# A segment loop with streamed weights: four stream buffers and 13 slices in place of five and 14, and the output columns split 256 + 384

## The chip, the cores and the metric

The kernel runs on one core of one Trainium2 chip. The metric is the device time of one execution in microseconds. TensorE (PE) multiplies and writes to PSUM, VectorE (DVE) and ScalarE (ACT) copy and compute, GpSimd (POOL) does a little, and SyncE (SP) and ScalarE issue the DMA transfers, which run on 16 DMA engines.

## The reference

`x` has 2048 rows of 640. Part A cuts it into 64 segments of 32 rows and carries 8 rows of memory from one segment to the next, so the segments form a chain:

```python
for s in range(n_seg):
    h = jnp.concatenate([mem, xs], axis=1)        # 8 + 32 rows
    q, k, v = h @ Wq, h @ Wk, h @ Wv              # each 640 -> 32 heads x 192
    p = softmax(where(mask, q k^T * scale, -1e9)) # 40 x 40 per head
    o = (p v) @ Wo                                # 6144 -> 640
    mem = o[:, :M, :]                             # the next segment's memory
    outs.append(o[:, M:, :])
```

Part B is a local attention with window 8 and dilation 2 over all 2048 rows. The result is `g * a + (1 - g) * b` with a gate `g` for each row.

## The kernel before, in words

Three stages run one after the other. `part_b` computes part B and stores it to DRAM. `prepass` projects those rows of each segment that do not depend on the chain. `part_a` is the loop over 64 segments that this text is about; `part_z` at the end finishes some output rows of all segments.

The four weight matrices do not fit into on-chip memory. Most of them is resident. What is not is cut into slices of 128 x 1536 bf16 (384 KB), listed in `STREAM` (L15). A slice of a projection is named by matrix, column unit and row chunk: `("q", 1, 1)` is unit 1 (512 columns of each quarter) of row chunk 1 of `Wq`. The five row chunks are the five blocks of 128 of the 640 inputs. A slice `("oa", i)` or `("ob", i)` is a piece of `Wo`: `oa` is the part that makes the first output columns, `ob` the rest. In every segment all 14 slices are read again from a copy in DRAM (`wscr`). `get_unit` (L565) takes one of `WBUFS` buffers of the pool `wst` and issues the transfer on SyncE's queue (L569); the transfer waits until TensorE has done its last matmul on the slice that was in that buffer.

Within a segment the order of TensorE, ScalarE and VectorE is written out by hand. `project` (L768) adds up one unit over row chunks: for each chunk four matmuls of 512 columns that run side by side, one for each quarter of the columns. `m_qk(i, chunks)` does this for the units of q (even i) and k (odd i), `c_qk(i)` copies the sum out of PSUM on ScalarE, `t_qk` transposes it, `s_a` and `s_b` make scores, `m_v` and `c_v` do the units of v, and `pv_half(h)` multiplies by the values for one half of the heads. `o_group(part, i2)` (L927) does four matmuls side by side against `Wo`; twelve groups make one part.

At the end of a segment ScalarE copies the finished output to `whi` (L1032 for the first part, L1040 for the second), and `sel` (L948) picks the 8 memory rows out of it with one small matmul for each of the row chunks that the part covers (L953). VectorE copies them to `hT` for the next segment (L956). The first part covers three row chunks and the second two, so the next segment starts its first units with chunks 0, 1 and 2, before the second `sel` has been done. `tail` (L1045) starts the matmuls of `ps_a` for the 24 or so remaining rows; the start of `ps_a` is a handy mark of a segment. Between the halves ScalarE also issues the store of `oz_dram` (L1025), and after L1032 the load for the next segment (`load_z`, L753).

The large sums of a segment take turns in two PSUM banks: the pool `psm` has two buffers under one tag (L748), and an allocation takes the one used before the last.

Of the kernel before, what the change touches and what calls it, by code (L numbers as in the profile page):

```python
# [11 lines left out]
F32 = mybir.dt.float32  # L12
I32 = mybir.dt.int32

STREAM = (("k", 0, 2), ("q", 1, 1), ("k", 1, 2), ("q", 2, 1), ("q", 2, 4), ("k", 2, 4), ("v", 0, 0), ("v", 1, 0), ("v", 1, 3),  # L15
          ("v", 2, 2), ("oa", 0), ("ob", 0), ("oa", 5), ("ob", 7))
N_EARLY = 22
N_COPY = 4
N_MID = 4
N_V = 8  # L20
N_LAST = 4
ZVB = 4
WBUFS = 5

_DEV = {"mode": "full"}

# [3 lines left out]
class _K:  # L30
# [466 lines left out]
    def weights_setup(self):  # L497
        nc, tc, KC = self.nc, self.tc, self.KC
        rest = []
        for m in "qkv":  # L500
            ks = sorted(range(KC), key=lambda kc: (len(self.units(m, 0, kc)) < 3, kc)) if m == "k" else range(KC)
            rest += [(m, J, kc) for kc in ks for J in range(4)]
        rest += [k for k in [("oa", i) for i in range(12)] + [("ob", i) for i in range(8)] if k not in STREAM]
        n = (0, N_EARLY, -N_MID - N_V - N_LAST, -N_V - N_LAST, -N_LAST, None)
        self.early, *self.late = [rest[n[x]:n[x + 1]] for x in range(5)]
        self.W = {m: W.rearrange("(c p) f -> p c f", p=128) for m, W in zip("qkv", (self.Wq, self.Wk, self.Wv))}
        self.wres = self.ctx.enter_context(tc.tile_pool(name="wres", bufs=1))
        self.res_tiles = {}
        self.ahead = {}
        self.after = mybir.DependencyInfo(mybir.DependencyClass.Sync, mybir.DependencyReason.DATA)  # L510
        self.wstream = self.ctx.enter_context(tc.tile_pool(name="wstream", bufs=WBUFS))
        self.wscr = dict(zip(STREAM, self.dram.tile([len(STREAM), 128, 1536], BF, name="wscr")))

    def tile_of(self, pool, k):
        n = 1536 if k[0] in ("oa", "ob") else 512 * len(self.units(*k))
        t = pool.tile([128, n], BF, name="w_" + "_".join(map(str, k)))
        self.res_tiles[k] = t if n < 1536 or k[0] in ("q", "k", "v") else t[:].rearrange(
            "p (c f) -> p c f", c=4 if k[0] == "oa" else 6)
        return t

    def load_res(self, k, t):
# [10 lines left out]

    def wo_slice(self, k, dst):

        n, f0, f1 = (4, 0, 384) if k[0] == "oa" else (6, 384, 640)
        src = self.Wo.rearrange("(c p) f -> p c f", p=128)[:, :, f0:f1]
        return dst.rearrange("p (c f) -> p c f", c=n), src[:, n * k[1]:n * k[1] + n]

    def wo_place(self, part, c):

        n = 4 if part == "oa" else 6
        return c // n, c % n

    def res(self, m, J, kc, c0, n):
# [175 lines left out]
    def part_a(self):  # L720
        nc, tc, KC, S = self.nc, self.tc, self.KC, self.S
        nseg = S // self.seg
        scale_a = float(self.Dh) ** (-0.5)
        ctx = ExitStack()
        with ctx:
# [19 lines left out]
            oTxs = [v.rearrange("p (c q) -> p c q", q=32) for v in V]  # L745
            a4 = ZB[:, 1536:1696]

            psm = ctx.enter_context(tc.tile_pool(name="psm", bufs=2, space=bass.MemoryType.PSUM, reuse_waits="tile"))  # L748
            psx = ctx.enter_context(tc.tile_pool(name="psx", bufs=2, space=bass.MemoryType.PSUM, reuse_waits="tile"))
            psS = ctx.enter_context(tc.tile_pool(name="psS", bufs=2, space=bass.MemoryType.PSUM, reuse_waits="tile"))  # L750

# [13 lines left out]
            for s in range(nseg):  # L765
                pqs, sts, pTs, pSs = {}, {}, {}, {}

                def project(ps, m, u, kcs):  # L768
                    for kc in kcs:
                        st = self.get_unit((m, u, kc)) if (m, u, kc) in STREAM else None  # L770
                        for j in range(4):
                            rhs = self.res(m, j, kc, 512 * u, 512) if st is None or j == 3 else st[:, 512 * j:512 * j + 512]
                            nc.tensor.matmul(ps[32 * j:32 * j + 32, :], lhsT=hT[:, kc, :], rhs=rhs, start=(kc == 0),  # L773
                                             stop=(kc == KC - 1), tile_position=(0, 32 * j), skip_group_check=True)

                def m_qk(i, kcs):
                    if i not in pqs:
                        pqs[i] = psS.tile([128, 2, 512], F32, tag="S", name="ps_qk")[:, 0, :] if i == 1 else \
                            psm.tile([128, 512], F32, tag="m", name="ps_qk")
                    project(pqs[i], ("q", "k")[i % 2], i // 2, kcs)  # L780

                def c_qk(i):
# [92 lines left out]

                def m_v(u, kcs=range(KC)):
                    if u not in pvs:
                        pvs[u] = psm.tile([128, 512], F32, tag="m", name="ps_v")
                    project(pvs[u], "v", u, kcs)

                def c_v(u):
# [43 lines left out]
                pso = {}  # L925

                def o_group(part, i2):  # L927
                    n = 384 if part == "oa" else 256
                    if i2 == 0:
                        pso[part] = psm.tile([128, 512], F32, tag="m", name="ps_wo")  # L930
                    for jj in range(4):
                        c = order[4 * i2 + jj]
                        J, g, t = c // 12, c // 3 % 4, c % 3
                        i, x = self.wo_place(part, c)
                        if (part, i) not in osl:
                            if s + 1 == nseg and sum(k[0] in ("oa", "ob") for k in STREAM) > WBUFS and i2 == 0 and part == "oa":
                                w = self.res_tiles[self.oz_free.pop()]
                                nc.sync.dma_start(w[:], self.wscr[part, i])
                            else:
                                w = self.get_unit((part, i))  # L940
                            osl[part, i] = w[:].rearrange("p (c f) -> p c f", c=4 if part == "oa" else 6)
                        nc.tensor.matmul(pso[part][32 * jj:32 * jj + 32, 0:n],  # L942
                                         lhsT=oTxs[2 * (g // 2) + J // 2][:, 6 * (J % 2) + 3 * (g % 2) + t, :],
                                         rhs=osl[part, i][:, x, :],
                                         start=(i2 == 0), stop=(i2 == 11),
                                         tile_position=(0, 32 * jj), skip_group_check=True)

                def sel(part, hT_next, pm):  # L948

                    m0, m1 = (0, 3) if part == "oa" else (3, KC)  # L950
                    p = 0 if part == "oa" else 1
                    for m in range(m0, m1):
                        nc.tensor.matmul(pm[:, p, 8 * (m - m0):8 * (m - m0) + 8], lhsT=whi[:, m * 128:(m + 1) * 128],  # L953
                                         rhs=self.sel_m[:], start=(m == m0), stop=(m == m1 - 1),
                                         skip_group_check=True)
                    nc.vector.tensor_copy(hT_next[:, m0:m1, 0:8], pm[:, p, 0:8 * (m1 - m0)].rearrange(  # L956
                        "p (m i) -> p m i", i=8))

                m_qk(0, (0, 1, 2))
                m_qk(1, (0, 1))  # L960
                if sel_b is not None:
                    sel_b()
                m_qk(1, (2,))
                if tail is not None:
                    tail()
                m_qk(0, (3, 4)); c_qk(0)
                m_qk(1, (3, 4)); c_qk(1)
                if store is not None:
                    store()
                m_qk(2, range(KC)); c_qk(2)  # L970
                m_qk(3, range(KC)); c_qk(3)
                m_qk(4, (0, 1))
                for i in range(4):
# [44 lines left out]
                c_z(0, pos, (1, 3), "aa")  # L1018
                c_z(0, pos, (0, 2), "dd")
                for i2 in range(6):  # L1020
                    o_group("oa", i2)
                pos = pv_half(1)
                c_x(1, pos, range(4), "adda")
                c_z(1, pos, range(4), "adad")
                nc.scalar.dma_start(self.oz_dram[s], zst)  # L1025
                if s + 1 == nseg:
                    self.sort_oz(0)
                for i2 in range(5):
                    o_group("ob", i2)
                for i2 in range(6, 12):  # L1030
                    o_group("oa", i2)
                nc.scalar.copy(whi[:, 0:384], pso["oa"][:, 0:384])  # L1032
# [56 lines left out]
    def part_z(self, psm, wo, tail):  # L1089
# [6 lines left out]
        for n in range(4):  # L1096
            b4 = self.res_tiles[free.pop(0)][:, 0:640]
            rows = lambda ap: ap.rearrange("(n s t) f -> n s t f", n=4, t=32)[n, :, 24:32, :]
            nc.scalar.dma_start(b4, rows(self.bsc_dram))
            for part, f0, nf in (("oa", 0, 384), ("ob", 384, 256)):  # L1100
                ps = psm.tile([128, 512], F32, tag="m", name="ps_z")
# [73 lines left out]
```

## Time and profile before

| What | Value |
|---|---|
| median of 3 runs | 1704.7 us (1703.22 to 1705.23) |
| the profiled execution | 1702.23 us, span 1700.5 us |
| TensorE busy | 1600.5 us, 94% of the span |
| granted TensorE clock, mean | 0.983 |
| read from HBM, written | 432.76 MB, 47.23 MB |
| transfers `wst<-wscr` | 896 of 384 KB, on SyncE's queue |
| the segment loop | from about 358 us to about 1640 us of the span |

The page gives busy times of the engines over the whole span and over 40 slices of it. Of the loop, 1282 us for 64 segments, a segment takes about 20 us. The chain of waits follows the work that ended last back to the start; a row with DMA in it is time between a transfer's issue and its landing. Idle time of an engine is listed with what ended it.

### The profile page before, as it was taken

What the parts mean: (1) busy time and instruction counts of PE and PEld (TensorE: products, weight loads), DVE (VectorE), ACT (ScalarE), POOL (GpSimd) and SP (SyncE); (2) the same over time, 40 slices, a digit from 0 to 9 for tenths busy, and PEclk for the clock granted to TensorE, in tenths of its full rate; (3) what the DMA queues carried; (4) which work ended last, traced back from release to release, by engine and by line L of the source; (5) the groups of instructions that cost most, each with busy time, mean ns of one, the idle gap of its engine ahead of it and who ended that gap; (6) DMA issues with size and microseconds to landing.
All of it is one profiled execution on the core that took longest, in us unless ns stands there. A gap on an engine that the chain in (4) does not pass through costs nothing.

```text
span 1700.5 us, 75713 instructions
## 1 busy us (share of the span) xinstructions
PE 1600.5 (94%) x33209; PEld 887.1 (52%) x33209; DVE 700.9 (41%) x2223; ACT 804.5 (47%) x2082; POOL 59.8 (4%) x124
## 2 busy tenths in 40 slices
PE   7887999989999999999999999999999999999989
PEld 4544544445555555555555555555555555555559
DVE  3665333234434444443344434434444434444430
ACT  3877422234444444444445444445454444454450
POOL 2030000000000000000000000000000000000000
PEclk9999899999999999999999999999999999999999
DMA  7798798889989999998999989999999999999981
GB/s 202 186 209 216 227 312 232 257 245 305 305 301 311 305 303 313 300 313 288 300 314 313 308 288 309 318 299 320 304 321 306 306 300 304 307 309 309 306 274 31
DMA packets 307608, 479.44 MB, mean 282 GB/s; under 512 B 100556, under 2 KB 186444, under 8 KB 307276
## 3 DMA queue, kind: packets, MB, share of 16 engines
q1 hardware_dynamic: 208144, 418.12, 75.8%
q10 hardware_dynamic: 99132, 56.46, 11.8%
q8 instruction: 260, 4.26, 1.0%
q14 instruction: 72, 0.59, 0.1%
HBM read 432.76 MB, written 47.23 MB: 282 GB/s over the span
## 4 chain that ended last, share of the span: by engine, by line
PE 85%; DMA 6%; ACT 3%; issue 3%; DVE 1%; SPq 1%; ACTq 0%; DVEq 0%
PE ps_qk L773 25%; PE ps_v L773 13%; PE ps_wo L942 13%; PE ps_pre L622 6%; PE ps_qkT L794 5%; PE ps_S L827 5%; PE ps_oT L899 3%; PE ps_z L1106 3%; PE ps_pre L652 3%; DMA wst<-wscr 2%; PE ps_S L859 2%; PE ps_bqk L236 2%; ACT ZB L1032 2%; DMA bqkT<-bqk_dram 1%; PE ps_mem L953 1%
## 5 line engine op out<-in xcount | busy, mean ns | idle before, releaser
L773 PEld LDWEIGHTS <-hT 128*32 128x32 bf16 x11520 | 277.2, 97 | 287.0 <-issue 18.6
L786 ACT CAST TZ<-ps_qk 128x512 bf16<-128x512 f32 x384 | 218.7, 587 | 315.3 <-PE ps_qk L773 315.3
L773 PE MATMUL ps_qk<-w_q,hT 128*32 128x512 bf16 x3264 | 267.9, 383 | 1.8 <-issue 1.6
L773 PE MATMUL ps_qk<-w_k,hT 128*32 128x512 bf16 x3264 | 266.0, 380 | 2.4 <-issue 2.0
L773 PE MATMUL ps_v<-w_v,hT 128*32 128x512 bf16 x3072 | 245.5, 384 | 0.0
L805 DVE COPY ZB<-ps_qkT 128x512 bf16<-128x512 bf16 (+1 forms) x256 | 91.0, 356 | 349.4 <-PE ps_qkT L794 253.7
L942 PEld LDWEIGHTS <-TZ 128*32 128x32 bf16 x6144 | 146.0, 96 | 110.4 <-ACT TZ L913 39.9
L883 DVE CAST TZ<-ps_v 128x512 bf16<-128x512 f32 (+1 forms) x256 | 136.9, 556 | 45.5 <-PE ps_v L773 45.5
L942 PE MATMUL ps_wo<-w_oa,TZ 128*32 128x384 bf16 x2560 | 147.4, 330 | 7.3 <-issue 6.8
L773 PE MATMUL ps_qk<-wst,hT 128*32 128x512 bf16 x1152 | 149.0, 381 | 0.8 <-DMA wst<-wscr 0.8
L913 ACT CAST TZ<-ps_oT 128x192 bf16<-128x192 f32 x256 | 75.9, 322 | 129.7 <-PE ps_oT L904 83.8
L942 PE MATMUL ps_wo<-w_ob,TZ 128*32 128x256 bf16 x2304 | 108.2, 275 | 14.0 <-issue 13.9
L956 DVE CAST hT<-ps_mem 128x24 bf16<-128x24 f32 x126 | 22.5, 179 | 227.6 <-PE ps_mem L953 227.6
L913 DVE CAST TZ<-ps_oT 128x192 bf16<-128x192 f32 x256 | 85.8, 355 | 57.7 <-PE ps_oT L904 55.8
L773 PE MATMUL ps_v<-wst,hT 128*32 128x512 bf16 x768 | 100.7, 387 | 9.0 <-DMA wst<-wscr 8.9
L794 PE MATMUL ps_qkT<-ident,TZ 128*128 128x128 bf16 x1536 | 107.3, 219 | 0.0
L794 PEld LDWEIGHTS <-TZ 128*128 128x128 bf16 x1536 | 88.6, 98 | 26.9 <-issue 26.9
L942 PE MATMUL ps_wo<-wst,TZ 128*32 128x256 bf16 (+1 forms) x1280 | 96.9, 302 | 4.8 <-issue 4.4
L845 ACT ACTIVATE TZ<-ps_S 32x224 bf16<-32x224 f32 x256 | 89.3, 349 | 13.0 <-PE ps_S L836 10.7
L845 ACT ACTIVATE ZB<-ps_S 32x224 bf16<-32x224 f32 x256 | 89.2, 348 | 13.0 <-PE ps_S L836 9.3
L754 POOL COPY TZ<-ZB 128x384 bf16<-128x384 bf16 x64 | 32.5, 507 | 1467.4 <-DMA ZB<-zpk_dram 565.1
L827 PE MATMUL ps_S<-ZB,TZ 64*128 64x160 bf16 (+1 forms) x704 | 78.1, 234 | 0.0
(135 smaller groups left out, 2037.6 us busy)
## 6 DMA issues: line engine op xcount, KB each, us to landing
wst<-wscr SPq DMA_DIRECT2D x896, 384.0 KB
zpk_dram<-ZS ACTq DMA_DIRECT2D x4, 3072.0 KB
ZB<-zpk_dram ACTq DMA_DIRECT2D x64, 192.0 KB
zpk_dram<-ZV ACTq DMA_DIRECT2D x32, 192.0 KB
TZ<-zpk_dram ACTq DMA_DIRECT2D x64, 96.0 KB
oz_dram<-TZ ACTq DMA_DIRECT2D x64, 96.0 KB
w_q<-in_A_Wq_dram SPq DMA_DIRECT2D x14, 384.0 KB
w_k<-in_A_Wk_dram SPq DMA_DIRECT2D x14, 384.0 KB
```

Of the source, the lines that this page charges most:

```text
L622: nc.tensor.matmul(ps[:], lhsT=weights(j, kc, 6 * Rp + 3 * r + t), rhs=zTi[:, kc, :], start=(kc == 0), stop=(kc == KC - 1))
L652: mm = nc.tensor.matmul(pss[g][:], lhsT=zTi[:, kc, 128 * st:128 * st + 128], rhs=weights(kc, g), start=(kc == 0), stop=(kc == KC - 1))
L773: nc.tensor.matmul(ps[32 * j:32 * j + 32, :], lhsT=hT[:, kc, :], rhs=rhs, start=(kc == 0), stop=(kc == KC - 1), tile_position=(0, 32 * j), ...
L786: nc.scalar.copy(sts[i], pqs[i][:])
L794: nc.tensor.transpose(pT[:, 128 * t:128 * t + 128], st[:, 128 * t:128 * t + 128], self.ident[:])
L805: nc.vector.tensor_copy(QTf[:, run[2]:run[2] + 4, run[3]:run[3] + n, :].rearrange("p b x i -> p x b i"), src.rearrange("p (x b i) -> p x b ...
L827: nc.tensor.matmul(grid(h, par)[:, :, 0:80].rearrange("p j (b r i) -> p j b r i", r=2, i=8)[:, :, :, r, :], lhsT=KTs[3 * R + t][k0:k1, :], ...
L845: nc.scalar.activation(E[ps], pSs[h][ps, :, 112 * j:112 * j + 112], ACT.Exp, scale=scale_a)
L883: nc.vector.tensor_copy(VU[u][:, f0:f1], pvs[u][:, f0:f1])
L899: nc.tensor.matmul(out[:, r, t, :], lhsT=Vt[6 * h + 3 * r + f0 // 128][ks, f0 % 128:f0 % 128 + f1 - f0], rhs=E[ks, par, 0:80].rearrange("p ...
L913: cp(oTxs[2 * h + j // 2][:, 6 * (j % 2):6 * (j % 2) + 6, :], pos[j][:, 0:240].rearrange("p (c q) -> p c q", q=40)[:, :, 8:40])
L942: nc.tensor.matmul(pso[part][32 * jj:32 * jj + 32, 0:n], lhsT=oTxs[2 * (g // 2) + J // 2][:, 6 * (J % 2) + 3 * (g % 2) + t, :], rhs=osl[pa ...
```

## The change

`WBUFS` goes from 5 to 4, and `STREAM` from 14 slices to 13, other ones, in the order in which a segment uses them. The output columns are split 256 + 384 (`oa` has two row chunks, `ob` three) where it was 384 + 256, so a slice of `oa` holds six blocks of `Wo` and one of `ob` four. In a segment the first six groups of `ob` now come before the second `pv_half`, then all twelve of `oa`, the copy of 256 columns, four groups of `ob`, the first `sel`, the last two groups of `ob`, and the copy of 384 columns.

Since the first `sel` gives only chunks 0 and 1, the next segment starts three units with these (q 0, k 0, and chunk 0 of q 1) before the second `sel`, where it started two units with chunks 0, 1, 2 and 0, 1. A unit may thus take its chunks in parts between other units; `done` counts them. The two PSUM banks get a tag each, `m` and `n`, and `bank` names which one a sum takes.

```diff
-STREAM = (("k", 0, 2), ("q", 1, 1), ("k", 1, 2), ("q", 2, 1), ("q", 2, 4), ("k", 2, 4), ("v", 0, 0), ("v", 1, 0), ("v", 1, 3),
-          ("v", 2, 2), ("oa", 0), ("ob", 0), ("oa", 5), ("ob", 7))
+STREAM = (("q", 1, 1), ("q", 1, 2), ("k", 1, 3), ("q", 2, 2), ("k", 2, 2), ("v", 0, 0), ("v", 1, 0), ("v", 1, 2), ("v", 2, 1),
+          ("ob", 0), ("oa", 0), ("oa", 5), ("ob", 8))
...
-WBUFS = 5
+WBUFS = 4
...
-        n, f0, f1 = (4, 0, 384) if k[0] == "oa" else (6, 384, 640)
+        n, f0, f1 = (6, 0, 256) if k[0] == "oa" else (4, 256, 640)
...
-            psm = ctx.enter_context(tc.tile_pool(name="psm", bufs=2, space=bass.MemoryType.PSUM, reuse_waits="tile"))
+            psm = ctx.enter_context(tc.tile_pool(name="psm", bufs=1, space=bass.MemoryType.PSUM, reuse_waits="tile"))
...
+                def bank(n, name):
+                    return psm.tile([128, 512], F32, tag="mn"[(s + n) % 2], name=name)
+
+                done = {}
+
                 def project(ps, m, u, kcs):
                     for kc in kcs:
+                        n = done[m, u] = done.get((m, u), 0) + 1
...
-                            nc.tensor.matmul(ps[32 * j:32 * j + 32, :], lhsT=hT[:, kc, :], rhs=rhs, start=(kc == 0),
-                                             stop=(kc == KC - 1), tile_position=(0, 32 * j), skip_group_check=True)
+                            nc.tensor.matmul(ps[32 * j:32 * j + 32, :], lhsT=hT[:, kc, :], rhs=rhs, start=(n == 1),
+                                             stop=(n == KC), tile_position=(0, 32 * j), skip_group_check=True)
...
-                            psm.tile([128, 512], F32, tag="m", name="ps_qk")
+                            bank(i == 2 or i == 4, "ps_qk")
...
-                        pvs[u] = psm.tile([128, 512], F32, tag="m", name="ps_v")
+                        pvs[u] = bank(u != 1, "ps_v")
...
-                        pso[part] = psm.tile([128, 512], F32, tag="m", name="ps_wo")
+                        pso[part] = bank(part == "oa", "ps_wo")
...
-                    m0, m1 = (0, 3) if part == "oa" else (3, KC)
+                    m0, m1 = (0, 2) if part == "oa" else (2, KC)
...
-                m_qk(0, (0, 1, 2))
+                m_qk(0, (0, 1))
                 m_qk(1, (0, 1))
+                m_qk(2, (0,))
                 if sel_b is not None:
                     sel_b()
-                m_qk(1, (2,))
+                m_qk(2, (1,))
                 if tail is not None:
                     tail()
-                m_qk(0, (3, 4)); c_qk(0)
-                m_qk(1, (3, 4)); c_qk(1)
+                m_qk(0, (2, 3, 4)); c_qk(0)
+                m_qk(1, (2, 3, 4)); c_qk(1)
...
-                m_qk(2, range(KC)); c_qk(2)
+                m_qk(2, (2, 3, 4)); c_qk(2)
...
                 for i2 in range(6):
-                    o_group("oa", i2)
+                    o_group("ob", i2)
                 pos = pv_half(1)
...
-                for i2 in range(5):
-                    o_group("ob", i2)
-                for i2 in range(6, 12):
+                for i2 in range(12):
                     o_group("oa", i2)
-                nc.scalar.copy(whi[:, 0:384], pso["oa"][:, 0:384])
+                nc.scalar.copy(whi[:, 0:256], pso["oa"][:, 0:256])
...
-                for i2 in range(5, 12):
+                for i2 in range(6, 12):
                     o_group("ob", i2)
-                    if i2 == 8 and s + 1 < nseg:
+                    if i2 == 9 and s + 1 < nseg:
                         sel("oa", hT_next, pm)
-                nc.scalar.copy(whi[:, 384:640], pso["ob"][:, 0:256])
+                nc.scalar.copy(whi[:, 256:640], pso["ob"][:, 0:384])
```

In `part_z` the two parts are 256 and 384 columns wide, in this order, in the banks `n` and `m`. The resident weights change in size to match: of the early loads some hold one unit more or fewer.

More of the change, by code (lines that the diff above doesn't have):

```diff
@@ L502, in weights_setup @@
             rest += [(m, J, kc) for kc in ks for J in range(4)]
-        rest += [k for k in [("oa", i) for i in range(12)] + [("ob", i) for i in range(8)] if k not in STREAM]
+        rest += [k for k in [("oa", i) for i in range(8)] + [("ob", i) for i in range(12)] if k not in STREAM]
         n = (0, N_EARLY, -N_MID - N_V - N_LAST, -N_V - N_LAST, -N_LAST, None)
@@ L517, in tile_of @@
         self.res_tiles[k] = t if n < 1536 or k[0] in ("q", "k", "v") else t[:].rearrange(
-            "p (c f) -> p c f", c=4 if k[0] == "oa" else 6)
+            "p (c f) -> p c f", c=6 if k[0] == "oa" else 4)
         return t
@@ L539, in wo_place @@
     def wo_place(self, part, c):
-        n = 4 if part == "oa" else 6
+        n = 6 if part == "oa" else 4
         return c // n, c % n
@@ L927, in o_group @@
                 def o_group(part, i2):
-                    n = 384 if part == "oa" else 256
+                    n = 256 if part == "oa" else 384
                     if i2 == 0:
-                        pso[part] = psm.tile([128, 512], F32, tag="m", name="ps_wo")
+                        pso[part] = bank(part == "oa", "ps_wo")
                     for jj in range(4):
@@ L940, in o_group @@
                                 w = self.get_unit((part, i))
-                            osl[part, i] = w[:].rearrange("p (c f) -> p c f", c=4 if part == "oa" else 6)
+                            osl[part, i] = w[:].rearrange("p (c f) -> p c f", c=6 if part == "oa" else 4)
                         nc.tensor.matmul(pso[part][32 * jj:32 * jj + 32, 0:n],
@@ L1099, in part_z @@
             nc.scalar.dma_start(b4, rows(self.bsc_dram))
-            for part, f0, nf in (("oa", 0, 384), ("ob", 384, 256)):
-                ps = psm.tile([128, 512], F32, tag="m", name="ps_z")
+            for part, f0, nf in (("oa", 0, 256), ("ob", 256, 384)):
+                ps = psm.tile([128, 512], F32, tag="m" if f0 else "n", name="ps_z")
                 for c in range(48):
```

## The prediction

> **What bounds the kernel now.** I read the page first (busy shares, the slices, the chain's shares), then the stretches of the loop, then the chain and the timelines of one segment, and last who waits on the DMA queue.
>
> ```profile
> PE 1600.5 (94%) x33209; PEld 887.1 (52%) x33209; DVE 700.9 (41%) x2223; ACT 804.5 (47%) x2082; POOL 59.8 (4%) x124
> PE   7887999989999999999999999999999999999989
> DMA  7798798889989999998999989999999999999981
> PE 85%; DMA 6%; ACT 3%; issue 3%; DVE 1%; SPq 1%; ACTq 0%; DVEq 0%
> 1000.00:1300.00 300.00, 291.21 (x6850) 160.45 (x6848) 127.68 (x461) 147.61 (x427) 7.61 (x15) 1.00 0.93 311
> ```
>
> The last row is a stretch of the loop: its length, busy time of TensorE, its weight loads, VectorE, ScalarE and GpSimd, then clock, DMA share and GB/s. TensorE bounds the loop (291 of 300 us busy, clock 1.00), but the DMA engines are busy 0.93 of the time: neither has much to spare. Taking the start of `ps_a` as the mark of a segment, the shortest of 62 segments lasts 19.06 us and the mean is 19.86. So 0.8 us a segment is lost to things that come and go. Most of it looks like this:
>
> ```profile
> 780.96 0.35 PE L942 MATMUL ps_wo<-w_oa,TZ 128*32 128x384 bf16 x4 [1.82 <-issue]
> q8 instruction: 260, 4.26, 1.0%
> ```
>
> TensorE waits for no semaphore here. The stalls of this kind stand 1792 TensorE instructions apart or a multiple of it, that is 7 x 256, and queue 8 moves the program in packets of 16 KB (260 packets for 66418 instructions: 256 each). I read them as late instruction fetches; aligned against the shortest segment they cost about 0.72 us of the 0.8.
>
> What even the shortest segment loses is one wait near its end:
>
> ```profile
> 1255.58 0.40 PE L942 MATMUL ps_wo<-wst,TZ 128*32 128x256 bf16 x6
> 1256.88 0.35 ACTq L1025 DMA_DIRECT2D oz_dram<-TZ  x1
> 1257.17 0.61 PE L942 MATMUL ps_wo<-w_ob,TZ 128*32 128x256 bf16 x16
> 1257.39 0.48 ACT L1032 CAST ZB<-ps_wo 128x384 bf16<-128x384 f32 x1 [0.54 <-PE ps_wo L942]
> 1257.93 0.23 PE L953 MATMUL ps_mem<-sel_m,ZB 128*128 128x8 bf16 x3
> ```
>
> Groups of four 256-column matmuls start 0.109 us apart (512 columns 0.216, 384 columns 0.163). The four groups that start at 1257.17 are over for the issue at 1257.17+4x0.109 = 1257.61, and the next matmul starts at 1257.93: 0.32 us of wait for the copy L1032.
>
> Last, the stream. SyncE waits for TensorE to free a buffer, hardly ever for anything else:
>
> ```profile
> SPq L569 <- PE ps_wo L942: 293.2, 250, 3.6
> SPq L569 <- PE ps_qk L773: 277.2, 300, 7.8
> SPq L569 <- DMA wst<-wscr: 18.3, 36, 2.7
> PE ps_v L773 <- DMA wst<-wscr: 8.9, 2, 5.6
> 809.18 7.14 DMA wst<-wscr
> ```
>
> A slice is issued 0.42 us after the last matmul on the buffer starts. From the issue to the last update of its semaphore the trace has, over 840 slices of the loop, 2.99 us at least, 4.69 in the median, 5.89 at the 95th percentile, 7.14 at most (the chain row at 809.18). From the last use of a buffer to the first use of the slice that comes into it there are 6.35 us in the tightest of 14 places. So TensorE waits for a slice only 0.03 us a segment.
>
> **The change, part by part**, for one of 63 segments.
>
> *Matmuls.* 445 of the same shapes, before and after, so nothing from their number; and the fetch boundaries fall as before.
>
> *The copy ahead of `sel`.* The last part finished ahead of the copy is now 256 columns wide, and the cover is four 384-column groups. From the rows: twelve 256-column groups from 1255.58, so the last starts at 1256.78 and ends at 1256.78+0.28 = 1257.06. ScalarE is still issuing the store L1025, to 1257.23: that becomes the late one. The copy of 256 columns (L1040's row: 0.37) ends at about 1257.62, `sel` starts at 1257.68 instead of 1257.93. TensorE is ready at 1256.78+0.109+4x0.163 = 1257.54, so 0.14 of wait stays. Gain 0.25; the next copy to `hT` has one chunk less ahead of the next segment (0.03 earlier) and one more at its second half (0.03 to 0.05 later). I take a gain of 0.23; its ends are 0.32 (no wait left) and 0.05 (the issue of L1025 ended up to 0.2 us later in other segments).
>
> *The three units begun early.* Sixteen matmuls of two units and four of a third stand ahead of the second `sel`, twenty before and after. The third unit's bank is freed by the copy of 384 columns: last group at 1257.68+0.30, its end 0.34 later, the copy 0.48 plus 0.1, ready at 1258.90; the matmul is due at 1257.68+0.475+4x0.216 = 1259.02. Hidden by the four groups, with 0.1 us to spare; if the cover is gone it costs what is missing, below 0.1 us. `c_qk(0)` and `c_qk(1)` come one and two groups later; the transposes that need them start 3.6 us into the segment, so nothing.
>
> *13 slices, four buffers.* The stream falls from 14x384 to 13x384 KB. But each slice has now the span of four, not five, slices. With the starts above I place the 13 in a segment of 18.83 us (from `ps_a`: 1.41, 2.70, 4.69, 5.76, 7.75, 8.84, 10.43, 11.28, 12.83, 14.62, 15.69, 16.95, 18.57) and take last use to first use, less 0.42. In that order, from ("q",1,2) on, the time that a slice may take is 5.06, 5.28, 6.03, 5.58, 5.91, 5.71, 5.31, 5.09, 4.65, 5.35, 4.83, 5.34 and, for ("q",1,1), 5.26. The tightest is ("ob",0), whose buffer is freed by ("v",0,0); 52% of the old latencies exceed its 4.65. Were latencies as before, the mean excess over the 13 budgets adds to 1.17 us a segment. Two things cut that. A wait at one slice gives the same time to the three already under way, so the excesses overlap: between all shared (1.17/4 = 0.29) and none. (The same sum for 14 slices and five buffers is 0.05, and 0.03 was lost.) And latency falls with load: where the last four issues took over 6.0 us its median was 4.42, under 5.3 it was 4.8 to 4.9; the new mean is about 5.8 to 6.0 against 5.67, so 0.1 us less, which makes the sum 0.94 and a quarter of it 0.24. I take 0.30, with ends 0.05 (latency falls by 0.4) and 0.65. SyncE's queue is in order: a late free holds up the next issue too, but it has 0.32 us of work per 1.4.
>
> The Trainium skill (DMA: Bandwidth & Descriptors, Anatomy of one DMA) fits a transfer as 2.0 us plus its bytes at 436 GB/s; that is an estimate of 2.9 us for 384 KB, near the fastest slice here (2.99) but far from the median (4.69). By it no budget would be missed and the term would be 0. The same page of the Trainium skill (Latency and other measured facts) says that a lighter load of the HBM makes the fixed part smaller; the rows by load agree in sign, with 0.4 us between the ends.
>
> *Fetch stalls.* 0.72 us a segment stay, since the instructions stay. About a quarter end in the stretch that gets shorter and eat its gain: 0.25x0.23, say 0.05; ends -0.1 and +0.1.
>
> *Ends of the program.* The last matmul part of `part_z` is 384 columns wide instead of 256, and the DVE step behind it some 0.1 us longer; in the last segment four loads of `oz` stand in SyncE's queue among slices with one buffer less, 0.3 us. The early weight loads change size (128 to 256 KB, 384 to 128, 256 to 384) in a stage with waits on SyncE's queue: within 3 us either way, taken as 0.
>
> **Sum.** -0.23 +0.30 +0.05 -0.03 (the old waits for slices, counted in the 0.30) = +0.09 us a segment, x63 = +5.7, with the ends +6. The profiled execution took 1702.2 us (span 1700.5), so 1708; the median shown is 1704.7, 2.5 above it, so 1710.
>
> **Rivals.** (1) *Waits stay small, the copy's gain shows: faster.* The slices are spaced more evenly (0.85 to 2.0 us apart, before 0.86 to 1.8), and 7% less traffic shortens queues. With the wait at 0.05 to 0.12 the segment is 0.06 to 0.18 shorter: 1693 to 1701. It decides at a wait of about 0.21 us a segment, that is at latencies some 0.25 us below the old. For it: the 4.42 median under light load. Against: fewer bytes also shorten the segment, so the load hardly falls: 14x384 KB and 504 KB of other transfers in 19.86 us are 296 KB per us, 13x384 and 504 in 18.83 to 19.9 us are 292 to 276. The 2.9 us of the Trainium skill (DMA: Bandwidth & Descriptors, Anatomy of one DMA) would lead to the same place: wait 0, 1691 to 1694. (2) *Cancelling*, wait 0.16 to 0.25: within 3.4 us, 1701 to 1708. (3) *Waits chain*: the excesses are not shared and the tail (5.9 us, 5%) hits every place: 0.65 a segment, +0.44x63 = 28 us, 1732. (4) *The cover of the third unit's bank fails*: at most 0.1x63 = 6 us more, inside the range of my forecast.
>
> **How the numbers follow.** 0.2% (3.4 us) is about what a measurement of this kernel can tell from no change. My forecast, slower by 4 to 20 us: 0.43. Rival 1: 0.32. Rival 2: 0.15. Rival 3: 0.10. Faster 0.32, same 0.15, slower 0.53. Both signs hold much of it: the forecast's own range is 1706 to 1725; the range that leaves out 2 in 10 is 1692 to 1731.
>
> **What the changed profile would show.** Right: "PE <- DMA wst<-wscr" waits grow from some 10 us to about 20 or more, first at L948's ("ob",0) and at ("oa",5) and ("v",2,1); the shortest segment falls to about 18.8 us while the mean rises to about 19.95; the wait for the whi copy (L1037) shrinks from 0.32 to about 0.14 and ScalarE's own queue (the `oz_dram` store) stands ahead of it; latencies of slices near 4.6. Wrong: latencies near 4.3 (then faster), a copy that starts as late as before, or stalls marked "issue" that grow or vanish with the load.

## The result: slower by 0.36%, and the profile after

Over 15 runs of each kernel the changed one takes 1712.25 us in the median (1703.71 to 1724.64), the kernel before 1706.11 us (1701.04 to 1712.43). The ratio is 1.0036, with a 95% interval of 1.0019 to 1.0053: about 6 us slower. The profiled execution took 1710.86 us, 8.6 us more than that of the kernel before (span 1709.1 against 1700.5).

The page of the changed kernel, its busy shares, the slices of the DMA engines and the shares of the chain:

```profile
PE 1597.3 (93%) x33193; PEld 890.9 (52%) x33209; DVE 701.7 (41%) x2223; ACT 810.3 (47%) x2082; POOL 59.5 (3%) x124
DMA  7798797978898899889988888988889889998881
PE 81%; DMA 9%; issue 3%; ACT 3%; DVE 2%; ACTq 1%; SPq 0%; DVEq 0%
```

The same stretch of the loop as before, again with TensorE, its weight loads, VectorE, ScalarE and GpSimd, then clock, DMA share and GB/s:

```profile
1000.00:1300.00 300.00, 288.57 (x6729) 161.14 (x6721) 125.91 (x451) 148.02 (x422) 7.61 (x15) 1.00 0.90 287
```

The DMA engines have less to do (0.90 for 0.93, 287 GB/s for 311; digits of 8 where there were 9), the clock is the same, and yet TensorE is busy for 2.6 us less of the 300 (2.2 in the mean of four such stretches from 400 to 1600 us), and transfers hold 9% of the chain where they held 6. Who TensorE waits for is in the view of its waits (total in us, number, longest):

```profile
PE ps_wo L948 <- issue: 31.6, 29, 1.9
PE ps_v L779 <- DMA wst<-wscr: 10.1, 4, 4.4
...
PE ps_wo L948 <- DMA wst<-wscr: 4.0, 6, 1.1
PE ps_qk L779 <- ACT ZB L1045: 3.7, 7, 1.2
...
PE ps_qk L779 <- DMA wst<-wscr: 2.3, 4, 1.1
```

Three things grew. Waits for slices (rows with DMA) add up to 16.4 us, where the kernel before had 9.7; the first and the last segment have 8.8 and 9.5 us of that, so between them it is 7.5 us where it was 0.3. The third unit waits for its bank (L1045), a wait that the kernel before does not have. And the "issue" stalls in the matmuls against `Wo`, late instruction fetches, went from 25.1 us to 31.6.

What the change promised is there too. The end of an undisturbed segment of the changed kernel, TensorE's matmuls and ScalarE's instructions in the timeline (start, length):

```profile
877.73 0.39 PE L948 MATMUL ps_wo<-wst,TZ 128*32 128x256 bf16 x6
877.94 0.82 PE L948 MATMUL ps_wo<-w_ob,TZ 128*32 128x384 bf16 x16
878.71 0.20 PE L959 MATMUL ps_mem<-sel_m,ZB 128*128 128x8 bf16 x2
...
877.92 0.32 ACTq L1032 DMA_DIRECT2D oz_dram<-TZ  x1
878.29 0.37 ACT L1037 CAST ZB<-ps_wo 128x256 bf16<-128x256 f32 x1 [0.39 <-PE ps_wo L948]
```

The four groups from 877.94 are over for the issue at 877.94+4x0.163 = 878.59; `sel` starts at 878.71. The wait for the copy is 0.12 us where it was 0.32, and ScalarE's issue of the `oz_dram` store (until 878.24) stands ahead of the copy. The shortest segment is 18.80 us where it was 19.06. But the mean went the other way, from 19.86 to 19.99 us.

The next table splits the segments of every profile of this study in the same way; the rows with three tiny matmuls belong to the last experiment. "Least" is the shortest segment, "mean" that of 62 segments. The other columns are ns a segment, each gap between two matmuls beyond that of the shortest segment: "slices" at the first matmul on a slice that starts within 70 ns of the slice's landing, "fetch" at the first matmul of a new block of 256 TensorE instructions, "bank" where the third unit waits for the copy. The columns do not add up to mean minus least exactly: what is lost at one place is in part won back behind it, and small gaps are in none of them.

| Kernel | least, us | mean, us | slices | fetch | bank | of before, 95% |
|---|---|---|---|---|---|---|
| before | 19.06 | 19.86 | 21 | 768 | 0 | 1 |
| changed | 18.80 | 19.99 | 138 | 891 | 66 | 1.0036 (1.0019 to 1.0053) |
| changed, load behind the copy | 18.80 | 19.89 | 143 | 918 | 0 | 1.0032 (1.0014 to 1.0050) |
| split and order only | 18.80 | 19.98 | 136 | 1007 | 1 | 1.0050 (1.0032 to 1.0069) |
| stream only | 19.05 | 19.74 | 84 | 587 | 0 | 1.0003 (0.9976 to 1.0029) |
| changed, no stream | 18.80 | 18.87 | 0 | 42 | 17 | one run |
| before, no stream | 19.05 | 19.08 | 0 | 29 | 0 | one run |
| changed, load behind, three tiny matmuls (41 first) | 18.80 | 19.93 | 136 | 945 | 0 | 1.0027 (1.0005 to 1.0050) |
| the same, 28 first | 18.80 | 19.87 | 103 | 929 | 0 | 1.0024 (1.0001 to 1.0046) |
| stream only, three tiny matmuls (41 first) | 19.05 | 19.88 | 176 | 663 | 0 | 1.0012 (0.9992 to 1.0031) |
| before, fetches held at 350, 414 | 19.05 | 19.50 | 5 | 454 | 0 | 0.9910 (0.9878 to 0.9942) |
| changed, fetches held at 350, 414 | 18.80 | 19.50 | 194 | 394 | 72 | 0.9871 (0.9827 to 0.9914) |
| the same, load behind the copy | 18.80 | 19.39 | 146 | 388 | 0 | 0.9846 (0.9814 to 0.9877) |
| the same, held at 299, 363, 427 | 19.21 | 20.30 | 72 | 1101 | 0 | 1.0188 (1.0154 to 1.0221) |

In the last row even the shortest segment has a fetch stall; against the shortest segment of the row above it, the fetch stalls are 1284 ns. One row is one profiled execution. That of the stream only was the fastest of its 12 runs (1686.6 us, median 1700.8), so its 587 may be low.

### The profile page after: what moved, and what is told of

The parts are those of the page before. It is cut to its first block, busy times and chain, and to the rows that moved or that the text cites. A ratio compares the mean times of both kernels' runs of the same rounds, so it can differ in the third digit from the quotient of the medians.

```text
span 1709.1 us, 75568 instructions
## 1 busy us (share of the span) xinstructions
PE 1597.3 (93%) x33193; PEld 890.9 (52%) x33209; DVE 701.7 (41%) x2223; ACT 810.3 (47%) x2082; POOL 59.5 (3%) x124
## 4 chain that ended last, share of the span: by engine, by line
PE 81%; DMA 9%; issue 3%; ACT 3%; DVE 2%; ACTq 1%; SPq 0%; DVEq 0%
PE ps_qk L779 24%; PE ps_v L779 12%; PE ps_wo L948 12%; DMA wst<-wscr 6%; PE ps_pre L622 6%; PE ps_qkT L800 5%; PE ps_S L833 4%; PE ps_z L1111 3%; PE ps_oT L905 3%; PE ps_pre L652 3%; PE ps_bqk L236 2%; PE ps_S L865 2%; PE ps_S L842 1%; DMA bqkT<-bqk_dram 1%; PE ps_mem L959 1%
## 5 line engine op out<-in xcount | busy, mean ns | idle before, releaser
L779 PEld LDWEIGHTS <-hT 128*32 128x32 bf16 x11520 | 282.2, 96 | 300.4 <-issue 31.8
L792 ACT CAST TZ<-ps_qk 128x512 bf16<-128x512 f32 x384 | 224.6, 585 | 307.6 <-PE ps_qk L779 297.3
L779 PE MATMUL ps_qk<-w_q,hT 128*32 128x512 bf16 x3264 | 286.3, 383 | 4.9 <-ACT ZB L1045 3.7
L779 PE MATMUL ps_qk<-w_k,hT 128*32 128x512 bf16 x3456 | 255.8, 380 | 2.8 <-issue 2.4
L948 PE MATMUL ps_wo<-w_ob,TZ 128*32 128x384 bf16 x2560 | 147.1, 328 | 7.6 <-issue 7.3
L779 PE MATMUL ps_qk<-wst,hT 128*32 128x512 bf16 x960 | 125.5, 384 | 2.6 <-DMA wst<-wscr 2.3
L962 DVE CAST hT<-ps_mem 128x16 bf16<-128x16 f32 x126 | 22.5, 179 | 228.1 <-PE ps_mem L959 228.1
L948 PE MATMUL ps_wo<-w_oa,TZ 128*32 128x256 bf16 x2304 | 82.8, 273 | 20.7 <-issue 19.5
```

Of the source, the lines that this page charges most:

```text
L792: nc.scalar.copy(sts[i], pqs[i][:])
L948: nc.tensor.matmul(pso[part][32 * jj:32 * jj + 32, 0:n], lhsT=oTxs[2 * (g // 2) + J // 2][:, 6 * (J % 2) + 3 * (g % 2) + t, :], rhs=osl[pa ...
```

## The experiments

My theory after reading the two profiles: the copy's gain (0.25 us a segment) is there, and it is given back in three places, waits for slices (0.12), the bank (0.07) and longer fetch stalls (0.12 and more). The rivals were that one of the three does it all, or that the fetch stalls differ by chance.

### The load behind the copy

The bank wait has a cause that the prediction did not see. The end of another segment of the changed kernel, ScalarE's part of the timeline, then TensorE's:

```profile
421.37 0.32 ACTq L1032 DMA_DIRECT2D oz_dram<-TZ  x1
421.73 0.37 ACT L1037 CAST ZB<-ps_wo 128x256 bf16<-128x256 f32 x1 [0.39 <-PE ps_wo L948]
421.75 2.51 ACTq L753 DMA_DIRECT2D ZB<-zpk_dram  x1
424.30 0.48 ACT L1045 CAST ZB<-ps_wo 128x384 bf16<-128x384 f32 x1 [2.20 <-issue]
...
423.07 0.60 PE L779 MATMUL ps_qk<-w_k,hT 128*32 128x512 bf16 x8
424.83 0.40 PE L779 MATMUL ps_qk<-w_q,hT 128*32 128x512 bf16 x4 [1.16 <-ACT ZB L1045]
```

L753, the issue of the load for the next segment, stands between the two copies in ScalarE's queue. It lasts 0.34 to 0.43 us in 43 of 62 segments, but here 2.51; the copy that frees the bank comes late, and the third unit with it.

```diff
                 nc.scalar.copy(whi[:, 0:256], pso["oa"][:, 0:256])
                 if s + 1 < nseg:
-                    load_z(s + 1)
...
                 nc.scalar.copy(whi[:, 256:640], pso["ob"][:, 0:384])
+                if s + 1 < nseg:
+                    load_z(s + 1)
```

> The changed kernel with one call moved: ScalarE issues the load for the next segment (L753) behind the copy of 384 columns (L1045), not ahead of it. Theory (the third unit's bank): in the profile of the changed kernel the issue of L753 lasts 0.34 us mostly but 1.1 to 2.5 us in 10 segments, L1045 stands behind it in ScalarE's queue, and the first matmul of the third unit waits 0.1 to 1.3 us, about 4 us in all. Moved, the wait is gone: 4 us faster than the changed kernel, about 1.001 of the kernel before. Rival (something else is late next, for instance the copy of the first sum behind a long issue): no gain, 1.0036 stays.

Measured: 1706.55 us, 1.0032 of before (1.0014 to 1.0050). In the profile the bank wait is gone (66 to 0 ns a segment), as the theory has it. The time does not show its 4 us: 1.0032 against 1.0036, and each has an interval of nearly 0.002 to either side. With the fetches held still (below) the same edit went from 0.9871 to 0.9846, again 4 us and again with intervals that overlap. So the mechanism is shown in the profile, its price is not resolved by the times.

### Each half of the change alone

Split and order alone, with the old number of buffers and slices:

```diff
-STREAM = (("q", 1, 1), ("q", 1, 2), ("k", 1, 3), ("q", 2, 2), ("k", 2, 2), ("v", 0, 0), ("v", 1, 0), ("v", 1, 2), ("v", 2, 1),
+STREAM = (("q", 1, 1), ("q", 1, 2), ("k", 1, 3), ("q", 2, 1), ("q", 2, 2), ("k", 2, 2), ("v", 0, 0), ("v", 1, 0), ("v", 1, 2), ("v", 2, 1),
...
-WBUFS = 4
+WBUFS = 5
```

> The changed kernel with five buffers and 14 streamed slices (one slice, q 2 1, added to its 13): the split and the order alone. The tightest place has 5.57 us for a slice, not 4.7. The least segment should be 18.8 us and waits for slices under 0.03 us a segment. Theory A (the longer fetch stalls of the changed kernel, 0.12 to 0.2 us a segment more than before, come with the four buffers or by chance): -15.6 us for the segment, +4 for the bank wait, about 0.993 of before (1694). Theory B (they come with the split: a shorter segment meets the same fetch times, so the gain of the copy is eaten): 0.999 to 1.001 of before.

The stream alone, in the kernel before:

```diff
-STREAM = (("k", 0, 2), ("q", 1, 1), ("k", 1, 2), ("q", 2, 1), ("q", 2, 4), ("k", 2, 4), ("v", 0, 0), ("v", 1, 0), ("v", 1, 3),
+STREAM = (("k", 0, 2), ("q", 1, 1), ("k", 1, 2), ("q", 2, 2), ("k", 2, 4), ("v", 0, 0), ("v", 1, 0), ("v", 1, 3),
...
-WBUFS = 5
+WBUFS = 4
```

> The kernel before with four buffers and 13 slices (q 2 2 in place of q 2 1 and q 2 4): the stream alone. Its tightest places have 4.5 to 4.7 us. The least segment stays 19.06 us. Theory A (four buffers bring the waits for slices, 0.12 us a segment, and delay nothing else): +7 us, 1.004 of before. Theory B (they bring the longer fetch stalls too): +15 to +20 us, 1.009 to 1.012. Rival (waits for slices overlap stalls that are there anyway): no change, within 0.002.

Measured: the split alone 1.0050 (1.0032 to 1.0069), slower although its shortest segment is 0.26 us shorter; the stream alone 1.0003 (0.9976 to 1.0029). The first is above both theories. The second is at the number of the rival, and below both theories. The waits of TensorE for its instructions in the `Wo` matmuls tell where it went; first the split alone, then the stream alone, and last the kernel before:

```profile
PE ps_wo L948 <- issue: 38.8, 33, 2.6
```

```profile
PE ps_wo L942 <- issue: 16.9, 24, 1.6
```

```profile
PE ps_wo L942 <- issue: 25.1, 26, 1.9
```

The split has longer fetch stalls (768 to 1007 ns a segment, +0.24, with as many slices), and the lighter stream shorter ones: 587 in the fast execution above, 663 in the padded one, whose time (1703.4 us) is near its median (1704.2), so 0.10 to 0.18 less. In the first case that eats the copy's gain of 0.25, and the waits for slices (+0.12) make the kernel slower. In the second it pays for the waits for slices (+0.06, and +0.16 in the padded one). The changed kernel has both: 891. The order of these sizes holds beyond single profiles: the new order with 13 slices has 891 to 945 in the four profiles with drifting places, the old order with 13 slices 587 and 663.

The waits for slices did not go as I had it either. The split alone, with five buffers, waits 136 ns a segment, as much as the changed kernel with four. Its 14 slices come in a shorter segment: the median time from issue to landing is 4.84 us and the 95th percentile 6.10 (before 4.69 and 5.89, changed 4.44 and 5.48), and its tightest place has 5.57 us where the kernel before has about 5.9 (6.35 less the 0.42 from last use to issue). Four buffers bring waits too: with the old order 84 and 176 ns in two profiles, where five have 21 and 5. I read all of them as the room for each slice against its latency; that is argued from these numbers.

### Without the stream

```diff
         if key in self.ahead:
             return self.ahead.pop(key)
+        self.held = getattr(self, "held", [])
+        if len(self.held) == WBUFS:
+            self.held.append(self.held.pop(0))
+            return self.held[-1]
         t = self.wstream.tile([128, 1536], BF, name="wst", tag="wst")
         self.nc.sync.dma_start(t[:], self.wscr[key])
+        self.held.append(t)
```

> The changed kernel without the stream: each buffer is loaded once and then used with its old contents, so 828 of 832 slice transfers are left out and the result is not the reference's. Theory (late instruction fetches are late because the DMA engines are busy with slices): the stalls at every 256th TensorE instruction all but vanish, the mean segment falls from 19.99 to about 18.85 us, 1638 us. Rival (a fetch is late by itself): only the waits for slices go, 0.12 us a segment, and perhaps the bank wait: 1698 to 1702 us.

> The kernel before without the stream: as in the changed kernel without the stream, each of the five buffers is loaded once and all later slice transfers are left out. Theory (the split does what it says, its 0.25 us a segment is lost only because instruction fetches come late beside the stream): with the fetches early in both, the difference of the least segments shows in the whole time: 15 to 16 us above the 1625.0 us of the changed kernel without the stream, 1640 to 1642. Rival (the gain is lost elsewhere): within 5 us of 1625.

Measured, one run each: 1625.0 us for the changed kernel without the stream, 1636.4 for the kernel before. The same stretch of the loop in the changed kernel without the stream, then in the kernel before without it:

```profile
1000.00:1300.00 300.00, 298.96 (x7080) 166.60 (x7072) 133.29 (x479) 155.76 (x446) 8.16 (x16) 1.00 0.11 31
1000.00:1300.00 300.00, 297.47 (x6946) 163.42 (x6934) 130.10 (x468) 152.14 (x437) 8.15 (x16) 1.00 0.12 31
```

TensorE is busy for 299 of 300 us, the fetch stalls fall from 891 to 42 ns a segment: late fetches are late because of the slices. The mean segment is the one expected (18.87 us for about 18.85); the time is 13 us below the 1638, because what stands ahead of the 62 segments (11 us) and behind them (5 us) got shorter as well. And then the change is worth 11.3 us, 0.21 us for each segment by the means (19.08 to 18.87). It is less than the 15 to 16 expected: some bank wait is left (17 ns a segment), and ahead of and behind the 62 segments 2 us are given back. The gain of the split is real, and it is lost beside the stream.

### Holding the fetches still

Where do the stalls stand? A new block of 256 instructions begins at places that drift through the segment, so the profiles sample all of them. Sums over 62 segments, by the place of the block's first matmul (445 in a segment, number 0 at the start of `ps_a`; the places named for the runs below are counted from two matmuls later):

| Place | before | changed | split only | stream only |
|---|---|---|---|---|
| 0 to 299 | 0.1 us | 1.2 us | 0.9 us | 0.4 us |
| 300 to 344 | 6.5 | 5.6 | 9.4 | 5.3 |
| 345 to 404 | 31.9 | 35.4 | 40.8 | 22.8 |
| 405 to 444 | 9.1 | 12.6 | 11.3 | 7.7 |

Nearly all of it is in the last third, where matmuls are shortest. The prediction had a quarter of it end in the stretch that the change shortens. So I made the number of TensorE instructions of a segment a multiple of 128 with tiny matmuls ahead of the first `sel`, whose result is overwritten by it, and set the places by more of them in the first segment. The first try added three and missed: the segment has 892 TensorE instructions, two of them semaphore events, and 898 let the places drift on.

```diff
                     p = 0 if part == "oa" else 1
+                    for x in range(0 if part == "ob" else 3 if s else 41):
+                        nc.tensor.matmul(pm[32 * (x % 3):32 * (x % 3) + 32, p, 0:8], lhsT=self.sel_x[:], rhs=self.sel_m[:],
+                                         start=True, stop=True, tile_position=(0, 32 * (x % 3)), skip_group_check=True)
                     for m in range(m0, m1):
```

> The changed kernel with the load behind the copy (L753 behind L1045) and three tiny matmuls ahead of the first sel of each segment, 41 in the first segment. A segment then has 448 matmuls = 896 TensorE instructions, 3.5 x 256, so every 256th instruction stands at the same two sets of places in all segments, spaced 64 matmuls over two of them; the 41 put them at matmuls 31 + 64 m, that is at 351 and 415 in the dense end of the segment. Theory (a stall is a fetch that is late for its place): by the mean stall of each place in the profiles so far the loss is 0.67 us a segment, not 0.90: -14 us against the kernel with the load behind, about 0.994 to 0.996 of before. Rival (stalls do not depend on the place, only on load): 1.003, and no difference to the next run.

> The same, with 28 tiny matmuls in the first segment, not 41: every 256th TensorE instruction at matmuls 44 + 64 m, that is at 300, 364 and 428. Theory (the place decides): 1.15 us a segment lost, +15 us against the kernel with the load behind, 1.011 to 1.013 of before, some 30 us slower than the run with places 351 and 415. Rival (only the load counts): 1.003, like that run.

> The kernel before with four buffers and 13 slices, and the same padding as the run with places 351 and 415. By the mean stalls of the places in the profiles of the kernel before and of this stream: 0.47 us a segment lost, not 0.62: -9 us against this stream without padding, 0.994 to 0.996 of before. Rival (only the load counts): 1.000.

Measured: 1.0027 (1.0005 to 1.0050), 1.0024 (1.0001 to 1.0046) and 1.0012 (0.9992 to 1.0031). No difference between the first two, as it must be when the places drift in both, and none of the last to the stream alone; the runs say nothing about the theory, only that three tiny matmuls cost nothing that can be measured. With two (`2 if s else 42`, or 29, and `x % 2`) the segment has 896:

> The changed kernel with the load behind the copy, and two tiny matmuls ahead of the first sel of each segment (42 in the first). The profiles count 892 TensorE instructions a segment, 2 of them semaphore events beside the 890 of the 445 matmuls, so three tiny matmuls made 898 and the places drifted by one matmul a segment; two make 896 = 3.5 x 256 and the places stand still, here at matmuls 30 + 64 m, that is 350 and 414. Mean stall by place over five profiles: 0.62 us a segment, 0.90 over all places. Theory (the place decides): -17 us against the kernel with the load behind, about 0.993 of before. Rival (only the load of the DMA engines counts, places even out): 1.003.

> The same with 29 tiny matmuls in the first segment: places 43 + 64 m, that is 299, 363 and 427 in all segments. Mean stall by place 1.21 us a segment. Theory (the place decides): +19 us, 1.014 of before, and 36 us slower than the run with places 350 and 414. Rival: 1.003, like that run.

> The kernel before with the two tiny matmuls ahead of the first sel (42 in the first segment), nothing else: places 350 and 414. Theory (the place decides): by the mean stalls of places in the profiles with this order, 0.43 us where the mean over all is 0.62, scaled to the 0.71 of the kernel before: 0.22 us a segment less, -14 us, 0.992 of before. Rival: 1.000.

> The changed kernel as it is, with the two tiny matmuls ahead of the first sel of each segment (42 in the first), so that every 256th TensorE instruction stands at places 350 and 414. Beside the kernel before with the same padding (0.991) it prices the change with the places of the fetches held still; beside the run with the load moved as well (0.985) it prices the third unit's bank. Theory (the bank wait costs what the profile of the changed kernel shows, 4 us): 0.987, that is 7 us faster than the kernel before with the same padding. Rival 1 (the load's place does not matter): 0.985. Rival 2 (the change gains nothing even with the places held): 0.991 or more.

Measured: with the places at 350 and 414 1674.6 us, 0.9846 (0.9814 to 0.9877); at 299, 363 and 427 1732.8 us, 1.0188 (1.0154 to 1.0221). The two kernels differ in 13 tiny matmuls of the first segment, and the times by 58 us. The costliest groups of TensorE in the first of them, with the idle time ahead of them and what ended it:

```profile
L779 PE MATMUL ps_qk<-w_k,hT 128*32 128x512 bf16 x3456 | 253.1, 379 | 0.4 <-DVE ZV L81 0.4
...
L948 PE MATMUL ps_wo<-wst,TZ 128*32 128x256 bf16 (+1 forms) x1280 | 94.1, 299 | 12.3 <-issue 6.6 <-DMA wst<-wscr 2.8 <-ACT TZ L926 1.4
L948 PE MATMUL ps_wo<-w_oa,TZ 128*32 128x256 bf16 x2304 | 84.0, 273 | 10.7 <-issue 10.5
```

and in the second:

```profile
L779 PE MATMUL ps_qk<-w_k,hT 128*32 128x512 bf16 x3456 | 263.7, 379 | 15.6 <-issue 14.7
...
L948 PE MATMUL ps_wo<-wst,TZ 128*32 128x256 bf16 (+1 forms) x1280 | 95.0, 302 | 4.0 <-DMA wst<-wscr 2.9 <-ACT TZ L926 0.7
L948 PE MATMUL ps_wo<-w_oa,TZ 128*32 128x256 bf16 x2304 | 90.9, 278 | 45.1 <-issue 45.1
```

The idle time marked "issue" is 17.1 us in these groups of the first and 59.8 in the second. The place decides; the size was underrated, -17 and +19 expected, -32 and +26 measured against 1.0032.

With the places held at 350 and 414 the kernel before takes 0.9910 (0.9878 to 0.9942) and the changed one 0.9871 (0.9827 to 0.9914), as expected (0.992 and 0.987). So the change that costs 0.36% while the places drift is no longer the slower kernel when they stand well. A gain is not shown: the intervals overlap, and the mean segment of the two profiles is the same, 19.50 us (that of the kernel before is the fastest of its six runs). With the load behind the copy the intervals just part: 0.9846 against 0.9910. That version, 1674.6 us, beats both kernels. It is good only for this count of instructions: with one matmul more a segment the places drifted, and the time was back at 1.0027.

## Why the prediction was right in sum and wrong in two terms

The forecast was +5.7 us, 1710 beside 1704.7; measured +6.1, inside its own range. That the sum came out is in part luck: two of its terms were off, in opposite directions. By its steps, in us a segment:

| Step | predicted | shown |
|---|---|---|
| the copy ahead of `sel` | -0.23 | -0.25 (least segment; 18.83 forecast, 18.80 found) |
| waits for slices, less the old | +0.27 | +0.12 |
| fetch stalls | +0.05, ends -0.1 and +0.1 | +0.12: split alone +0.24, lighter stream alone -0.10 and -0.18 in two profiles |
| the third unit's bank | 0, at most 0.1 | +0.07 |
| sum | +0.09 | +0.06 of these, +0.12 by the means |

- *The copy* was right down to what is late next, ScalarE's issue of the `oz_dram` store.
- *Waits for slices*: 2.3 times too large. The step that failed is "so 0.1 us less": the median latency fell by 0.25 us (4.69 to 4.44), the 95th percentile by 0.4. The budgets were right within 0.07 us (4.72 in the tightest place, 4.65 forecast). With the latencies of the changed kernel their mean excess adds to 0.55 us, not 0.94, and a quarter of it, the shared case, is the 0.14 that was waited. One reason is on record: the last four issues took 6.15 us in the mean, not 5.8 to 6.0, since the segment did not get shorter. That four buffers in place of five are what brings the waits is only half of it: the split alone, with five, waits as much. And of the three places named, ("v",2,1) waited 34 ns a segment, ("oa",5) 12 and ("ob",0), the tightest, none; ("k",1,3) waited most, 35. The fit of the Trainium skill that the prediction sets beside its sum (DMA: Bandwidth & Descriptors, Anatomy of one DMA) is given there for transfers that GpSimd issues, and the slices are issued by SyncE. By the prediction's own point, waits of 0.21 us at latencies 0.25 below the old, rival 1 should then have won, and it would have, had the other two terms been as small as I took them.
- *Fetch stalls* is the term of the sum that was too small, just above its upper end: "About a quarter end in the stretch that gets shorter and eat its gain". Nearly all of them stand in the last third of the segment. For places 380 to 420 the 128 matmuls ahead took 3.65 to 4.06 us in the shortest segment before and 3.37 to 3.63 after, 0.35 less in the mean, from the copy and from twelve 256-column groups that now stand in one row. The block's packet starts 1.7 us (mean, before) after the block ahead of it was begun, and its first matmul comes 2.2 us after that at the earliest: a stretch under some 4 us stalls on average, and what it gets shorter is waited for. The places 365 to 429 have 0.29 us less in the mean; at 3.48 blocks a segment that is an estimate of 0.15 of the 0.24. Of the rest, 0.05 stands at places 300 to 344, whose 128 matmuls take as long in both kernels (within 0.01 us), so the shorter stretch is not the whole cause; the rest is open.
- *The bank* (rival 4) happened for a reason that it did not name: not the copy's own length, but the issue of L753 ahead of it. Its bound of 6 us held: 66 ns x 62 = 4.1.

So the total came out right because a term that was 0.15 too large stood beside two that were 0.14 too small together. Of the signs, the shortest segment (18.80 us), the mean (19.99) and the wait for the copy (0.12) came as forecast. TensorE's waits for slices went from 10 to 16 us, fewer than "20 or more", latencies fell between what the text had as right (4.6) and wrong (4.3), and the stalls marked "issue" grew (25.1 to 31.6 us), which it had named as a sign of being wrong.

## What to carry to other kernels

Before a wait is removed, ask what limits the stretch that becomes shorter: here the engine's own instruction fetch did in part, and a gain of 0.25 us a segment, 16 us in all, was lost beside the stream and worth 11 us without it. In an unrolled loop on a busy DMA, count the instructions of an engine in one pass against 256: stalls marked "issue" at a fixed distance are the sign, and a few idle instructions can move them. A DMA issue between two copies on one queue is not a constant 0.33 us either (here up to 2.51); put the copy that others wait for ahead of it. And compare a profiled execution with the median of its runs before its stalls are taken as typical.

## What the runs showed of the hardware

- *A fetch whose block ahead begins 0.15 us later can start 2.0 us later.* With the load behind the copy and the places held at 350, the block ahead of the stalled one begins 11.97 us into the segment, and the packet starts 0.70 us after that (median of 31); held at 363, the block begins at 12.12, and the packet starts 2.55 us after it. From there to the first matmul both take 2.2 us at best, 2.57 and 2.33 in the median. The stall follows the packet's delay with a correlation of 0.88 and 0.98. Three or four slices are in flight in both cases. Without the stream the mean delay of all blocks falls from 1.54 to 0.32 us. So slices delay a fetch; that it waits behind them, and that its place between them decides, is how I read it, and in which order the DMA engines take them no run shows. The Trainium skill (DMA: Bandwidth & Descriptors, Queues, rings and completion order) says that each DMA engine takes its queues in turn, a whole packet at a time, which would fit.
- *How well fetches are hidden depends on the load.* The Trainium skill (Runtime: NRT & Kernel Launch, Instruction fetch mechanics) has blocks of 16 KB, 256 instructions, and calls the cost of crossing into the next one mostly hidden. The blocks agree with the packets of queue 8. Hidden they are without the stream (42 ns a segment); beside it 0.4 to 1.3 us of 20 are lost to them.
- *A DMA issue can last longer where it meets a fetch.* L753's issue on ScalarE took at most 0.43 us in the 36 segments of the changed kernel in which no packet of queue 8 was under way, and up to 2.51 us in the other 26 (median 0.87); those over 0.5 us end 0.38 us (median) after the packet. But meeting a packet is not enough. With the load behind the copy the same issue met one in 21 segments and was longer than 0.5 us in two, and ScalarE's other issues in the loop of the changed kernel met 80 packets, and none of them lasted over 0.59 us. All issues of slices over 0.5 us on SyncE met a packet, but these are 31 of 208 that did. What the long ones share beyond the packet is open; it was not tried.
